# A fused attention and mixer kernel on one core: the row maxima of a query group by four products into one PSUM bank and one reduction, six visits to the value products in a group instead of seven, and the output products at other places

## The chip, the cores and the metric

One core of a Trainium2 chip runs the whole kernel. The metric is the device time of one execution in microseconds (us), the median of several runs. The engines are named as in the profile: PE (TensorE, with PEld for its weight loads), DVE (VectorE), ACT (ScalarE), POOL (GpSimd), and SP, which here issues DMAs only.

## The reference

`x` has 2048 tokens of 448 features; there are 16 query heads of 28 features, one shared key head and one shared value head.

```python
def _A_ref(x, wq, wk, wv, wo):
    q = (x @ wq).reshape(B, S, H, Dh).transpose(0, 2, 1, 3)
    k = x @ wk
    v = x @ wv
    scores = jnp.einsum("bhqd,bkd->bhqk", q, k) * (Dh ** -0.5)
    p = _softmax(scores, axis=-1)
    o = jnp.einsum("bhqk,bkd->bhqd", p, v)
    return o.transpose(0, 2, 1, 3).reshape(B, S, H * Dh) @ wo
def _B_ref(x, w1, w2, w3, w4):
    h = _gelu(_layernorm(x) @ w1)
    # four quarters of h, shifted by +1, -1, +2, -2 tokens, side by side: hs
    x1 = x + hs @ w2
    return x1 + _gelu(_layernorm(x1) @ w3) @ w4
g = _sigmoid((x * gate_w).sum(-1, keepdims=True))
out = g * _A_ref(x, ...) + (1 - g) * _B_ref(x, ...)
```

## The kernel before, in words

Three stages follow one another. In the first, the projections q, k, v and the first half of the mixer are computed. In the second, the mixer's wide MLP runs (`w3_part`, `w4_part`): for each block of 512 tokens, 14 slices of hidden features. The third stage is attention, and nearly all of the change lies there.

**Attention.** The work is cut into 16 groups `u` (4 blocks of 512 tokens by 4 groups of 4 heads). A group has 64 steps `at` = 4 kt + j: one per key tile `kt` (16 tiles of 128 keys) and head `j`. Step `at` is one score product on PE, called S below (S0 to S63 of a group): 128 keys by 512 queries into one PSUM bank. ACT then takes the exponential of that bank (one ACTIVATE) into an SBUF tile `p`.

**Values.** For each key tile, four products of `p` with the values accumulate into the bank `pv`, which stands apart from the others; they work side by side in four column strips of 32. They are not issued after each key tile but in visits: `VISITS = {kt: (lo, hi)}` says that after the scores of key tile `kt`, the value products of the tiles lo to hi - 1 (negative ones: of the group before) are issued. In the trace a key tile of values is eight MATMULs of line 870.

**Banks.** The score products go round seven PSUM banks in a fixed order: `bank()` takes the first of a list and puts it at the end. S therefore waits until whatever used its bank last has been read: by ACT, or by DVE where the bank held something else.

**Other PE work between the scores.** Three kinds of it:

- Output products (`wo_job`, W below): for the group before, four jobs of three products of 448 columns. A job takes the first bank off the list, holds it through its three products, puts it at the end of the list, and DVE then adds the bank to the output tile `ot` (line 824). `pump()` issues one product; `WO_AT` lists the steps at which it is called (`WO_LAST` in the last group).
- In the first group, four jobs of the same form (`w4_job`, at the steps `W4_AT`) finish the MLP's last hidden slice for the last 512 tokens. DVE adds their banks to `x1` (line 847). It needs `x1` of these tokens already multiplied by 1 - g, which POOL does in `weigh_x1(NT - 4, NT)` after it has cast and split the output weights (`woh`, `wol`, lines 830 and 831) that a DMA brings.
- Maxima (M below): a lower estimate of each query's largest score, taken over the first 32 keys, is subtracted in the scores of the next group through two extra rows of `qs`. Four products (one per 128 tokens, 128 columns each: 4 heads by 32 keys, `max_part`) each take a bank, and DVE reduces each (line 211). After the fourth, `max_end` does three small DVE operations, and SP sends the result to `qs` by four DMAs. For group 0 this is done within the second stage (`fills`).

After the last value product of a group, DVE copies `pv` to `o` (line 778), a DMA round trip spreads the reciprocal sums (`recip`), and `norm` (DVE, then POOL, lines 796 to 800) makes the operand of the output products.

All engines execute in the order in which the code is written.

Of the kernel before, what the change touches and what calls it, by code (L numbers as in the profile page):

```python
# [9 lines left out]
F32 = mybir.dt.float32  # L10
# [3 lines left out]
AX = mybir.AxisListType  # L14
PSUM = bass.MemoryType.PSUM

P = 128
# [3 lines left out]
DH = 28  # L21
# [3 lines left out]
NT = S // P  # L25
# [7 lines left out]
MK = 32  # L33
# [8 lines left out]
def gated_mix_kernel(  # L42
# [12 lines left out]
    nc = tc.nc  # L55
# [141 lines left out]
    NU = NB * NG  # L197
    q_of = {}
    qr_of, qh_of, ql_of = {}, {}, {}
    mx_of = {}  # L200
# [2 lines left out]
    def max_tile(name):  # L203
        return psA.tile([P, 512], F32, tag="mx", bufs=1, name=name)

    def max_part(u, t, tile_of):
        if t == 0:
            mx_of[u] = late.tile([P, 4, 4], F32, tag="mr", bufs=2, name=f"mr_{u}")
        ps = tile_of(f"m_{u}_{t}")[:, 0:4 * MK].rearrange("p (j k) -> p j k", j=4)
        nc.tensor.matmul(ps, qh_of[u][:, t * P:(t + 1) * P], khd[0:4 * DH], start=True, stop=True)  # L210
        nc.vector.reduce_max(mx_of[u][:, :, t], ps, axis=AX.X)  # L211

    def max_full(u, tile_of):
        mr = late.tile([P, 4, 4], F32, tag="mr", bufs=2, name=f"mf_{u}")
# [11 lines left out]
    def max_end(u):  # L226
        mr = mx_of.pop(u).rearrange("p j t -> p (j t)")
        mc = late.tile([P, 32], F32R, tag="mc", bufs=2, name=f"mc_{u}")
        nc.vector.tensor_scalar(mc[:, 0:16], mr, -1.0, None, op0=ALU.mult)
        nc.vector.scalar_tensor_tensor(mc[:, 16:32], mr, -1.0, f32(mc)[:, 0:16],  # L230
                                       op0=ALU.mult, op1=ALU.subtract)
        mrow = late.tile([P, 32], F32, tag="mrow", bufs=2, name=f"mrow_{u}")
        nc.vector.transpose(mrow, f32(mc))
        for p in range(4):
            nc.sync.dma_start(f32(qs_of[u % 2])[96:98, :, :].rearrange("k j (t p q) -> k p (j t) q", p=4, q=32)[:, p],
                              mrow[32 * p:32 * p + 32, :])
# [4 lines left out]
    with tc.tile_pool(name="s1b", bufs=1) as s1b, \  # L241
# [327 lines left out]
        late = ctx.enter_context(tc.tile_pool(name="late", bufs=1, side="right", reuse_waits="tile"))  # L569
        khd = late.tile([P, 4, MK], F32R, name="khd")  # L570
# [73 lines left out]
    with tc.tile_pool(name="s2", bufs=1, reuse_waits="tile") as s2, \  # L644
# [2 lines left out]
            for n in range(n0, n1):  # L647
                nc.gpsimd.tensor_scalar(x1[:, n, :], x1[:, n, :], gi[:, n:n + 1], None, op0=ALU.mult)

        fills = [lambda t=t: max_part(0, t, max_tile if t % 2 else misc_tile) for t in range(4)]  # L650
        fills += [lambda: max_end(0)]

        def fill():
            if fills:
# [84 lines left out]
    with tc.tile_pool(name="s3", bufs=1, reuse_waits="tile") as s3, \  # L739
# [121 lines left out]
        p_of, pv_of, sums, norms = {}, {}, [], []  # L861
# [10 lines left out]
            if kt == NT - 1 and u < NU - 1:  # L872
                sums.append(sums_begin(u, pv_of.pop(u)))

        WO_AT = (33, 36, 37, 40, 43, 44, 48, 50, 52, 53, 54, 55)
        M_AT = (5, 11, 17, 22)
        M_FIRST = (20, 29, 36, 40)
        W4_AT = (22, 29, 36, 37, 38, 41, 49, 50, 51, 54, 58, 61)
        WO_LAST = (36, 37, 38, 49, 50, 51)
        VISITS = {0: (-2, 0), 2: (0, 2), 4: (2, 4), 6: (4, 6), 8: (6, 8), 11: (8, 11), 14: (11, 14)}  # L880

        for k in range(NU * NT + 1):
            u, kt = divmod(k, NT)
            if k < NU * NT:
                if kt == 8 and 0 < u < NU - 1:
                    q_rows(u + 1)
                if kt == 13 and u + 2 < NU:
                    q_begin(u + 2)
                    q_fetch(u + 3)
                if kt == WO_AT[0] // 4 and u > 0:  # L890
                    for t in range(4):
                        jobs.append(wo_job(u - 1, t))
                if k == 0:
                    for t in range(4):
                        jobs.append(w4_job(t))
                pump_at = W4_AT if u == 0 else WO_AT if u < NU - 1 else WO_LAST
                p_of[k] = []
                for j in range(4):
                    n, at = 4 * k + j, 4 * kt + j
                    ps = bank(f"s_{n}")  # L900
                    nc.tensor.matmul(ps, kS[0:98, kt * P:(kt + 1) * P], q_of[u][0:98, j, :], start=True, stop=True)  # L901
                    p = s3.tile([P, 512], F32, tag="p", bufs=PB, name=f"p_{n}")
                    nc.scalar.activation(p, ps, AF.Exp, scale=SCALE)  # L903
                    p_of[k].append(p)
                    if at in pump_at:
                        pump()
                    if at == 12 and sums:
                        norms.append(recip(*sums.pop()))
                    if at == 27 and norms:
                        norm(*norms.pop())  # L910
                    m_at = M_AT if u else M_FIRST
                    if u + 1 < NU and at in m_at:
                        t = m_at.index(at)
                        max_part(u + 1, t, bank)
                        if t == 3:
                            max_end(u + 1)
            if k == NU * NT:
                while current[0] or jobs:
                    pump()
            lo, hi = VISITS.get(kt, (0, 0))  # L920
            for kk in range(u * NT + lo, u * NT + hi):
                if kk >= 0:
                    pv_group(kk)
        assert not sums and not norms

        u = NU - 1
# [155 lines left out]
```

## Time and profile before

| what | value |
|---|---|
| median of 3 runs | 957.29 us (957.19 to 958.32) |
| the profiled execution | 958.51 us, of which the span of its instructions 956.6 us |
| mean granted TensorE clock | 0.996 of full speed |
| busy over the span | PE 99%, ACT 68%, PEld 66%, DVE 29%, POOL 12% |
| attention's first score product, last exponential's start | 399.2 us, 940.6 us |

Times in the views are us from the start of the span. A PE row that is busy is not PE at its peak: matmuls are pipelined, so the distance from one start to the next is what a product costs, and the duration in the row is longer.

### The profile page before, as it was taken

How to read it: one execution, taken by the hardware profiler on the slowest of the kernel's cores; microseconds unless marked ns; L12 is line 12 of the kernel's file. 1: busy time of each engine (PE TensorE's matmuls, PEld its weight loads, DVE VectorE, ACT ScalarE, POOL GpSimd, SP SyncE). 2: the span in 40 equal slices, each digit the busy share in tenths (PEclk: the TensorE clock that was granted, in tenths of full speed). 3: DMA queues.
4: the chain of work that ended last, by engine and by line, in shares of the span. 5: the costliest groups of instructions: out<-in, count | busy, mean ns of one | idle time of the engine just before them, and what ended most of it. 6: DMA issues, size and time to landing. Idle time of an engine off the chain costs nothing.

```text
span 956.6 us, 13529 instructions
## 1 busy us (share of the span) xinstructions
PE 947.0 (99%) x5175; PEld 630.7 (66%) x5175; DVE 278.4 (29%) x573; ACT 648.3 (68%) x1266; POOL 116.5 (12%) x140
## 2 busy tenths in 40 slices
PE   9999999999999999999999999999999999999996
PEld 6788888888888888755555555455555555555543
DVE  5564454533423411221222122122221212212112
ACT  5542453322221222499999999999999999999994
POOL 3353300200002400040000000000000000000000
PEclk9999999999999999999999999999999999999998
DMA  9823452301300300111011021101111101210101
GB/s 308 279 70 90 131 165 84 84 10 29 83 2 1 83 1 10 38 51 42 23 40 48 16 79 51 38 21 46 52 52 40 52 16 37 89 42 13 31 13 42
DMA packets 45239, 57.33 MB, mean 60 GB/s; under 512 B 9856, under 2 KB 27968, under 8 KB 45168
## 3 DMA queue, kind: packets, MB, share of 16 engines
q1 hardware_dynamic: 41936, 50.47, 18.4%
q10 hardware_dynamic: 3168, 5.70, 1.7%
q8 instruction: 42, 0.69, 0.3%
q14 instruction: 29, 0.24, 0.1%
q0 software_dynamic: 64, 0.23, 0.1%
HBM read 32.19 MB, written 11.67 MB: 46 GB/s over the span
## 4 chain that ended last, share of the span: by engine, by line
PE 98%; DMA 1%; DVE 0%; ACT 0%; issue 0%; POOL 0%; POOLq 0%; ACTq 0%; SPq 0%
PE bank L901 28%; PE pv L870 25%; PE acc L678 5%; PE acc L680 5%; PE acc L679 5%; PE g L134 4%; PE g L135 4%; PE g L136 4%; PE bank L816 1%; PE bank L814 1%; PE bank L812 1%; PE g L137 1%; PE g L138 1%; PE h L134 1%; PE h L135 1%; PE h L136 1%
## 5 line engine op out<-in xcount | busy, mean ns | idle before, releaser
L903 ACT ACTIVATE p<-bank 128x512 f32<-128x512 f32 x1024 | 511.3, 643 | 32.9 <-PE bank L901 30.6
L901 PE MATMUL bank<-qs,kS 98*128 98x512 f32 x1024 | 305.8, 410 | 0.0
L901 PEld LDWEIGHTS bank<-qs,kS 98*128 98x128 f32 x1024 | 184.0, 189 | 134.3 <-issue 93.1
L870 PE MATMUL pv<-p,vext 128*32 128x512 f32 x2048 | 243.1, 598 | 0.0
L668 ACT ACTIVATE gh<-g 128x512 fp32r<-128x512 f32 x55 | 32.9, 598 | 184.5 <-PE g L138 184.5
L870 PEld LDWEIGHTS pv<-p,vext 128*32 128x32 f32 x2048 | 59.0, 109 | 114.6 <-issue 108.2
L670 DVE TENSOR_TENSOR gl<-gf,gh 128x512 fp32r<-128x512 f32 x55 | 38.2, 695 | 164.6 <-ACT gf L669 160.3
L678 PE MATMUL acc<-w4h,gh 128*128 128x448 f32 x220 | 80.2, 365 | 0.0
L680 PE MATMUL acc<-w4h,gl 128*128 128x448 f32 x220 | 80.0, 364 | 0.0
L679 PE MATMUL acc<-w4l,gh 128*128 128x448 f32 x220 | 79.9, 363 | 0.0
L824 DVE SCALAR_TENSOR_TENSOR ot<-bank,gg,ot 128x448 f32<-128x448 f32 x44 | 30.0, 684 | 146.2 <-ACT p L903 91.2
L799 POOL CAST onh<-on 128x512 fp32r<-128x512 f32 x15 | 9.1, 610 | 471.1 <-DVE on L796 471.1
L134 PE MATMUL g<-ah,w3h 128*128 128x512 f32 x168 | 65.8, 392 | 0.0
L135 PE MATMUL g<-al,w3h 128*128 128x512 f32 x168 | 65.7, 391 | 0.0
L136 PE MATMUL g<-ah,w3l 128*128 128x512 f32 x168 | 65.7, 391 | 0.0
L211 DVE TENSOR_REDUCE mr<-bank 128x4 f32<-128x128 f32 x60 | 17.6, 293 | 108.1 <-PE bank L210 108.1
L679 PEld LDWEIGHTS acc<-w4l,gh 128*128 128x128 f32 x220 | 41.3, 188 | 4.2
L678 PEld LDWEIGHTS acc<-w4h,gh 128*128 128x128 f32 x220 | 41.3, 188 | 4.2
L680 PEld LDWEIGHTS acc<-w4h,gl 128*128 128x128 f32 x220 | 41.3, 188 | 3.1
L778 DVE COPY o<-pv 128x512 f32<-128x512 f32 x15 | 10.4, 692 | 99.4 <-PE pv L870 99.4
L136 PEld LDWEIGHTS g<-ah,w3l 128*128 128x128 f32 x168 | 31.5, 188 | 7.0
L135 PEld LDWEIGHTS g<-al,w3h 128*128 128x128 f32 x168 | 31.5, 188 | 5.7
(195 smaller groups left out, 962.6 us busy)
## 6 DMA issues: line engine op xcount, KB each, us to landing
qs<-qh SPq DMA_DIRECT2D x32, 224.0 KB
qd<-qf ACTq DMA_DIRECT2D x16, 256.0 KB
rb<-rd SPq DMA_DIRECT2D x15, 256.0 KB
x<-in_x_dram SPq DMA_DIRECT2D x4, 896.0 KB
xd<-xt SPq DMA_DIRECT2D x16, 224.0 KB
w34raw<-in_w_dram SPq DMA_DIRECT2D x7, 512.0 KB
qr<-qd SPq DMA_DIRECT2D x16, 224.0 KB
qs<-ql SPq DMA_DIRECT2D x16, 224.0 KB
```

The costliest lines, as they stand in the source:

```text
L134: nc.tensor.matmul(ps, wh[:, c, :], ah[:, c, :], start=(c == 0), stop=False)
L135: nc.tensor.matmul(ps, wh[:, c, :], al[:, c, :], start=False, stop=False)
L136: nc.tensor.matmul(ps, wl[:, c, :], ah[:, c, :], start=False, stop=False)
L668: nc.scalar.activation(gh, ps, AF.Gelu_apprx_tanh)
L670: nc.vector.tensor_sub(gl, gf, f32(gh))
L678: nc.tensor.matmul(ps, gh[:, tok], w4h[i][:, k, :], start=(f == 0), stop=False)
L679: nc.tensor.matmul(ps, gh[:, tok], w4l[i][:, k, :], start=False, stop=False)
L680: nc.tensor.matmul(ps, gl[:, tok], w4h[i][:, k, :], start=False, stop=(f == stop))
L824: nc.vector.scalar_tensor_tensor(ot_of[n], ps, gg[:, n:n + 1], before, op0=ALU.mult, op1=ALU.add)
L870: nc.tensor.matmul(pv[32 * j:32 * j + 32, :], vext[:, kt, :], ps[j], start=(kt == 0), stop=(kt == NT - 1), tile_position=(0, 32 * j))
L901: nc.tensor.matmul(ps, kS[0:98, kt * P:(kt + 1) * P], q_of[u][0:98, j, :], start=True, stop=True)
L903: nc.scalar.activation(p, ps, AF.Exp, scale=SCALE)
```

## The change

The four maxima products of a group now stand in a row, each writing a quarter of the same bank, and one DVE reduction with 4 x 4 x 32 elements per partition reads them all; `max_end` follows at once. They stand at step 38 in every group. In the second stage, too, the five fill pieces become one.

```diff
-    def max_part(u, t, tile_of):
-        if t == 0:
-            mx_of[u] = late.tile([P, 4, 4], F32, tag="mr", bufs=2, name=f"mr_{u}")
-        ps = tile_of(f"m_{u}_{t}")[:, 0:4 * MK].rearrange("p (j k) -> p j k", j=4)
-        nc.tensor.matmul(ps, qh_of[u][:, t * P:(t + 1) * P], khd[0:4 * DH], start=True, stop=True)
-        nc.vector.reduce_max(mx_of[u][:, :, t], ps, axis=AX.X)
+    def max_first(u, tile_of):
+        mx_of[u] = late.tile([P, 4, 4], F32, tag="mr", bufs=2, name=f"mr_{u}")
+        ps = tile_of(f"m_{u}")[:, 0:16 * MK]
+        for t in range(4):
+            nc.tensor.matmul(ps[:, 4 * MK * t:4 * MK * (t + 1)], qh_of[u][:, t * P:(t + 1) * P], khd[0:4 * DH],
+                             start=True, stop=True)
+        nc.vector.reduce_max(mx_of[u].rearrange("p j t -> p t j"),
+                             ps.rearrange("p (t j k) -> p t j k", t=4, j=4), axis=AX.X)
+        max_end(u)
...
-        fills = [lambda t=t: max_part(0, t, max_tile if t % 2 else misc_tile) for t in range(4)]
-        fills += [lambda: max_end(0)]
+        fills = [lambda: max_first(0, misc_tile)]
...
-        WO_AT = (33, 36, 37, 40, 43, 44, 48, 50, 52, 53, 54, 55)
-        M_AT = (5, 11, 17, 22)
-        M_FIRST = (20, 29, 36, 40)
-        W4_AT = (22, 29, 36, 37, 38, 41, 49, 50, 51, 54, 58, 61)
+        WO_AT = (36, 37, 37, 38, 38, 39, 49, 50, 50, 63, 63, 63)
+        W4_AT = (22, 23, 24, 37, 38, 39, 49, 50, 51, 61, 62, 63)
         WO_LAST = (36, 37, 38, 49, 50, 51)
-        VISITS = {0: (-2, 0), 2: (0, 2), 4: (2, 4), 6: (4, 6), 8: (6, 8), 11: (8, 11), 14: (11, 14)}
+        M_AT = 38
+        VISITS = {1: (-3, 0), 3: (0, 3), 5: (3, 5), 7: (5, 7), 11: (7, 10), 14: (10, 13)}
...
-                    if at in pump_at:
+                    for _ in range(pump_at.count(at)):
                         pump()
-                    if at == 12 and sums:
+                    if at == 14 and sums:
                         norms.append(recip(*sums.pop()))
-                    if at == 27 and norms:
+                    if at == 29 and norms:
                         norm(*norms.pop())
...
+                    if u + 1 < NU and at == M_AT:
+                        max_first(u + 1, bank)
...
-            lo, hi = VISITS.get(kt, (0, 0))
+            lo, hi = VISITS.get(kt, (0, 0)) if k < NU * NT else (-3, 0)
```

Lines shift a little: the score product is line 902 after the change, the value product 872, the output products 814 to 818, the products of `w4_job` 843 to 847 and its DVE addition 849.

**First place: PE in group 0, around the last product of the first `w4_job`.** In the rows, `bank_0` to `bank_6` are the seven banks, `gl_late` is an operand of the third product of such a job, and the brackets name the engines waited for. Before:

```order
L901 MATMUL bank_6_3224<-qs0_1049,kS_75 128x512
L845 MATMUL bank_3_3221<-w4h_6_1504,gl_late_3174 128x448
L210 MATMUL bank_0_3218<-khd_1047,qh_1_3229 128x128
L901 MATMUL bank_1_3219<-qs0_1049,kS_75 128x512 [waits Activation_49]
L841 MATMUL bank_2_3220<-w4h_6_1504,gh_late_3173 128x448 [waits Activation_49]
L901 MATMUL bank_4_3222<-qs0_1049,kS_75 128x512 [waits Activation_49]
L843 MATMUL bank_2_3220<-w4l_6_1505,gh_late_3173 128x448
L901 MATMUL bank_5_3223<-qs0_1049,kS_75 128x512 [waits Activation_49]
L901 MATMUL bank_6_3224<-qs0_1049,kS_75 128x512 [waits Activation_49]
L210 MATMUL bank_3_3221<-khd_1047,qh_1_3229 128x128 [waits DVE_49]
```

After:

```order
L902 MATMUL bank_4_3216<-qs0_1049,kS_75 128x512
L847 MATMUL bank_2_3214<-w4h_6_1504,gl_late_3168 128x448
L902 MATMUL bank_5_3217<-qs0_1049,kS_75 128x512
L902 MATMUL bank_6_3218<-qs0_1049,kS_75 128x512 [waits Activation_49]
L902 MATMUL bank_0_3212<-qs0_1049,kS_75 128x512 [waits Activation_49]
L902 MATMUL bank_1_3213<-qs0_1049,kS_75 128x512 [waits Activation_49]
L902 MATMUL bank_3_3215<-qs0_1049,kS_75 128x512 [waits Activation_49]
L902 MATMUL bank_4_3216<-qs0_1049,kS_75 128x512 [waits Activation_49]
L902 MATMUL bank_2_3214<-qs0_1049,kS_75 128x512 [waits DVE_49]
```

The job's third product moved from behind S36 to behind S24, and the bank that it filled is asked for again by S31 (the last row), where before a maxima product behind S40 was the first to ask for it.

**Second place: PE in a middle group, around the maxima.** The names are those of group 10, whose maxima are for group 11. Before, one of the four maxima products:

```order
L901 MATMUL bank_4_3222<-qs0_1049,kS_75 128x512
L901 MATMUL bank_0_3218<-qs0_1049,kS_75 128x512
L901 MATMUL bank_1_3219<-qs0_1049,kS_75 128x512 [waits Activation_49]
L210 MATMUL bank_6_3224<-khd_1047,qh_11_6348 128x128 [waits Activation_49]
L901 MATMUL bank_2_3220<-qs0_1049,kS_75 128x512 [waits DVE_49]
L901 MATMUL bank_3_3221<-qs0_1049,kS_75 128x512 [waits Activation_49]
```

After, from the second product of the second output job (its bank is `bank_2`) at S38 to S46:

```order
L816 MATMUL bank_2_3214<-wol_3211,onh_9_6506 128x448
L210 MATMUL bank_0_3212<-khd_1047,qh_11_6311 128x128 [waits Activation_49]
L210 MATMUL bank_0_3212<-khd_1047,qh_11_6311 128x128 x3
L902 MATMUL bank_5_3217<-qs0_1049,kS_75 128x512 [waits Activation_49]
L818 MATMUL bank_2_3214<-woh_3210,onl_9_6507 128x448
L902 MATMUL bank_1_3213<-qs0_1049,kS_75 128x512 [waits Activation_49]
L902 MATMUL bank_3_3215<-qs0_1049,kS_75 128x512 [waits Activation_49]
L902 MATMUL bank_6_3218<-qs0_1049,kS_75 128x512 [waits DVE_49]
L902 MATMUL bank_4_3216<-qs0_1049,kS_75 128x512 [waits Activation_49]
L902 MATMUL bank_0_3212<-qs0_1049,kS_75 128x512 [waits DVE_49]
L902 MATMUL bank_5_3217<-qs0_1049,kS_75 128x512 [waits Activation_49]
L902 MATMUL bank_2_3214<-qs0_1049,kS_75 128x512 [waits DVE_49]
```

Three banks in eight steps now come back from DVE: the first job's at S42, the maxima's at S44 and the second job's at S46 (the last row).

**Third place: DVE in the same group.** Before, with `good`, `rr` and `on` belonging to the normalisation of group 9:

```order
L211 TENSOR_REDUCE mr_11_6440<-bank_2_3220 128x4 [waits PE_49]
L211 TENSOR_REDUCE mr_11_6440<-bank_6_3224 128x4 [waits PE_49]
L229 TENSOR_SCALAR mc_11_6524<-mr_11_6440 128x16 [waits DVE_49]
L230 SCALAR_TENSOR_TENSOR mc_11_6524<-mr_11_6440,mc_11_6524 128x16 [waits DVE_49]
L233 STREAM_TRANSPOSE mrow_11_6527<-mc_11_6524 128x32 [waits DMAHW5_49,DVE_49]
L796 TENSOR_TENSOR on_9_6548<-o_9_6430,rb_9_6480 128x512 [waits DMAHW3_49,Pool_49]
L824 SCALAR_TENSOR_TENSOR ot_8_6285<-bank_0_3218,gg_78,ot_8_6285 128x448 [waits PE_49,Activation_49]
L824 SCALAR_TENSOR_TENSOR ot_9_6311<-bank_6_3224,gg_78,ot_9_6311 128x448 [waits PE_49,Activation_49]
```

After:

```order
L798 TENSOR_TENSOR on_9_6504<-o_9_6406,rb_9_6436 128x512 [waits DMAHW3_49,DVE_49,Pool_49]
L826 SCALAR_TENSOR_TENSOR ot_8_6230<-bank_6_3218,gg_78,ot_8_6230 128x448 [waits PE_49,Activation_49]
L212 TENSOR_REDUCE mr_11_6554<-bank_0_3212 128x4x4 [waits PE_49,Activation_49]
L232 TENSOR_SCALAR mc_11_6560<-mr_11_6554 128x16 [waits DVE_49]
L233 SCALAR_TENSOR_TENSOR mc_11_6560<-mr_11_6554,mc_11_6560 128x16 [waits DVE_49]
L236 STREAM_TRANSPOSE mrow_11_6563<-mc_11_6560 128x32 [waits DMAHW7_49,DVE_49]
L826 SCALAR_TENSOR_TENSOR ot_9_6256<-bank_2_3214,gg_78,ot_9_6256 128x448 [waits PE_49]
```

The reduction and the three operations of `max_end` now stand between the additions of the first and the second output job, where before they stood ahead of both.

More of the change, by code (lines that the diff above doesn't have):

```diff
@@ L904, in gated_mix_kernel @@
                     p_of[k].append(p)
-                    if at in pump_at:
+                    for _ in range(pump_at.count(at)):
                         pump()
-                    if at == 12 and sums:
+                    if at == 14 and sums:
                         norms.append(recip(*sums.pop()))
-                    if at == 27 and norms:
+                    if at == 29 and norms:
                         norm(*norms.pop())
[L911 to L916, printed above, removed]
+                    if u + 1 < NU and at == M_AT:
+                        max_first(u + 1, bank)
             if k == NU * NT:
```

## The prediction

> **What bounds the kernel now.** I read the page first (engines, chain), then the lines of the attention stage, and then the timeline of one group.
>
> ```profile
> PE 947.0 (99%) x5175; PEld 630.7 (66%) x5175; DVE 278.4 (29%) x573; ACT 648.3 (68%) x1266; POOL 116.5 (12%) x140
> ...
> PE 98%; DMA 1%; DVE 0%; ACT 0%; issue 0%; POOL 0%; POOLq 0%; ACTq 0%; SPq 0%
> ...
> L903 ACT ACTIVATE p<-bank 128x512 f32<-128x512 f32 x1024 | 511.3, 643 | 32.9 <-PE bank L901 30.6
> L901 PE MATMUL bank<-qs,kS 98*128 98x512 f32 x1022 | 305.3, 410 | 0.0
> ```
>
> The chain is PE almost throughout. In attention, ACT's idle time before the exponentials (32.9 us) is nearly all put down to PE (30.6), and PE's own idle time is nil: PE sets the pace, ACT follows closely. So whatever PE issues counts in full, and whatever makes PE wait counts too. One group, from the timeline:
>
> ```profile
> 604.80 0.69 DVE L778 COPY o<-pv 128x512 f32<-128x512 f32 x1 [6.93 <-PE pv L870]
> 612.69 0.96 PE L901 MATMUL bank<-qs,kS 98*128 98x512 f32 x3
> 613.49 0.23 PE L210 MATMUL bank<-khd,qh 112*128 112x128 f32 x1
> 613.55 1.37 PE L901 MATMUL bank<-qs,kS 98*128 98x512 f32 x5
> 613.75 0.29 DVE L211 TENSOR_REDUCE mr<-bank 128x4 f32<-128x128 f32 x1 [3.02 <-PE bank L210]
> 614.08 0.17 DVE L229 TENSOR_SCALAR mc<-mr 128x16 fp32r<-128x16 f32 x1
> 614.29 0.17 DVE L230 SCALAR_TENSOR_TENSOR mc<-mr,mc 128x16 fp32r<-128x16 f32 x1
> 614.50 0.21 DVE L233 STREAM_TRANSPOSE mrow<-mc 128x32 f32<-128x32 f32 x1
> 614.63 0.65 DVE L796 TENSOR_TENSOR on<-o,rb 128x512 f32<-128x512 f32 x1
> 623.85 0.37 PE L816 MATMUL bank<-woh,onl 128*128 128x448 f32 x1
> 624.05 0.96 PE L901 MATMUL bank<-qs,kS 98*128 98x512 f32 x3
> 624.33 0.68 DVE L824 SCALAR_TENSOR_TENSOR ot<-bank,gg,ot 128x448 f32<-128x448 f32 x1 [1.57 <-PE bank L816]
> 624.51 0.19 PEld L901 LDWEIGHTS bank<-qs,kS 98*128 98x128 f32 x1 [0.27 <-ACT p L903]
> 624.94 2.78 PE L870 MATMUL pv<-p,vext 128*32 128x512 f32 x24
> 627.65 0.50 PE L901 MATMUL bank<-qs,kS 98*128 98x512 f32 x1
> 629.99 0.40 PE L901 MATMUL bank<-qs,kS 98*128 98x512 f32 x1
> 630.87 1.10 PE L901 MATMUL bank<-qs,kS 98*128 98x512 f32 x4
> 634.61 2.13 PE L901 MATMUL bank<-qs,kS 98*128 98x512 f32 x8
> 636.67 1.92 PE L870 MATMUL pv<-p,vext 128*32 128x512 f32 x16
> 638.53 0.73 PE L901 MATMUL bank<-qs,kS 98*128 98x512 f32 x2
> 638.74 0.69 DVE L778 COPY o<-pv 128x512 f32<-128x512 f32 x1 [6.92 <-PE pv L870]
> ```
>
> A group takes 638.74 - 604.80 = 33.94 us. Prices, start to start: a score product (1.10 - 0.40)/3 = 0.233. An output product 624.05 - 623.85 = 0.20. A visit: two key tiles take 638.53 - 636.67 = 1.86, three 627.65 - 624.94 = 2.71, so 0.85 a tile and 0.16 for any visit; the eight scores ahead, 636.67 - 634.61 = 2.06, are 0.19 more than 8 x 0.233. **A visit's fixed price is 0.35 us.** A maxima product between scores: from the last score before it (612.69 + 0.96 - 0.40 = 613.25) to the last after it (613.55 + 1.37 - 0.40 = 614.52) it is 1.27, five scores are 1.165, so 0.105.
>
> **The change, part by part.**
>
> *Visits.* Seven a group (six in the first) and one at the end were 112; six a group (five in the first) and one at the end are 96. Each group gains 0.35.
>
> *Maxima in a row.* The trace has no two such products together. Bounds for one behind another: the 0.06 from 613.49 to 613.55 below, a score's 0.233 above. I take 0.11, the same product's price between scores, its nearest row. [...]
>
> ```profile
> L210 PEld LDWEIGHTS bank<-khd,qh 112*128 112x128 f32 x60 | 11.3, 188 | 2.1
> ```
>
> So four in a row cost what four apart cost, within 0.02. Were a whole load of 188 ns paid for each, the sum would be 15 x 3 x 0.078 = 3.5 us higher. [...]
>
> *One reduction of 512 elements.* Not in the trace. Bounds: 0.29 (row of 613.75, 128 elements) and four times that, 1.17. I take 0.69, DVE's copy of 512 elements out of PSUM (row of 604.80). DVE has the time; what matters is who queues behind it. That is the addition of the second output job, whose bank S46 wants. From the first maxima product, at 0: fourth product 0.33; reduction from 0.33 + 0.26 (613.49 to 613.75) = 0.59 to 1.28; the three operations of max_end and the hand-over, 0.59 (from 614.04, the end of the reduction, to 614.63), to 1.87; addition 0.68, to 2.55; 0.05 to answer the wait and 0.10 for the weight load, so 2.70. PE without a wait: S39 at 0.44, the job's third product at 0.67, S40 at 0.88, S46 at 0.88 + 6 x 0.233 = 2.28. **S46 waits 0.42 us.** Behind it on PE are S47, a visit and all the rest. The maxima's own bank (S44, 1.81 against 1.28 + 0.15) and the first job's are back in time. Their price per product drops out of this wait: it delays both sides.
>
> A wait of 0.1 at the old S47 goes: its weight load came at 624.51, held up by ACT, so that the product could start at 624.61, not at 624.05 + 2 x 0.233 = 624.52. Middle groups: -0.35 + 0.42 - 0.1 + 0.05 (one old maxima product stood ahead of a visit and cost less) = +0.02, **14 groups +0.3**, in effect nothing.
>
> *The first group.* Its rows:
>
> ```profile
> 399.20 3.53 PE L901 MATMUL bank<-qs,kS 98*128 98x512 f32 x12
> 417.44 0.37 PE L845 MATMUL bank<-w4h,gl_late 128*128 128x448 f32 x1
> ...
> 399.63 17.83 ACT L903 ACTIVATE p<-bank 128x512 f32<-128x512 f32 x36 [2.69 <-PE bank L901]
> ...
> 411.00 1.68 POOL L830 CAST woh<-woraw 128x1792 fp32r<-128x1792 f32 x1 [12.63 <-DMA woraw<-in_wo_dram]
> 412.76 4.04 POOL L831 TENSOR_TENSOR wol<-woraw,woh 128x1792 fp32r<-128x1792 f32 x1
> 416.78 5.56 POOL L648 TENSOR_SCALAR x<-x,gi 128x448 f32<-128x448 f32 x4
> ...
> 418.22 0.68 DVE L847 SCALAR_TENSOR_TENSOR x<-bank,gi,x 128x448 f32<-128x448 f32 x1 [4.04 <-POOL x L648]
> ```
>
> Before, the first late job ended at 417.44, and its addition started at 418.22, when POOL had weighed the first x1 tile (416.78 + 5.56/4 = 418.17). POOL hangs on a DMA, not on PE, and the change moves nothing ahead of it on SP or POOL. Now the job ends behind S24. Where is that? Scores now run 16 in a stretch; from S9 on they take ACT's pace, 17.83/36 = 0.49, as the stretched 3.53 of the twelve shows. S8 at 399.20 + 1.87, S15 at 404.3 (S9 a little early), a visit of three tiles, S16 at 407.4; seven scores and two job products, 2.4 with the step to the visit, its two tiles 1.86: S24 at 411.7. S25 to S30 follow, and S31, on the job's bank, would start 0.1 + 0.2 + 7 x 0.233 later, at 413.6. The addition cannot start before 418.2; the bank is back at 418.22 + 0.68 + 0.15 = 419.05. **S31 waits 5.5 us**, and PE, in order, does nothing else. The first group: -0.35 (a visit), -0.85 (a tile moved to the end), +1.0 (S12 to S15 at ACT's pace, 4 x 0.26), +5.5, and, with small waits exchanged, +0.1: **+5.4**.
>
> *The last group and the end.* Visits after key tiles 7 and 11 leave 16 scores and three products between them, with no maxima to slow PE. S47 would be at 0.34 + 14 x 0.233 + 0.6 = 4.2 from S32, but its bank holds S40's scores, whose exponential starts 0.6 + 8 x 0.48 = 4.4 and is over, with 0.15, at 5.25: a wait of 1.0, less 0.35 for the visit. At the end three tiles instead of two follow the last scores, +0.85. **Together +1.5.**
>
> *Second stage.* One fill instead of five: the same four products on PE, DVE busy 1.3 us in one piece; the slice's gl is used two slices later, so it is covered. Nothing. Were that cover gone, 1 us once.
>
> *PE's clock behind the 5.5 us.* PE idles nowhere for so long before; the nearest rows are the tail, by windows (PEclk is the figure behind the engines):
>
> ```profile
> 943.00:945.00 2.00, 1.37 (x6) 0.84 (x6) 1.10 (x5) 0.91 (x6) 0.00 (x0) 1.00 0.00 0
> 945.00:946.00 1.00, 0.69 (x3) 0.50 (x4) 0.87 (x6) 0.50 (x3) 0.00 (x0) 1.00 0.00 0
> 946.00:948.00 2.00, 2.00 (x8) 1.57 (x7) 1.23 (x4) 0.27 (x1) 0.00 (x0) 0.52 0.00 0
> 948.00:950.00 2.00, 2.00 (x8) 1.55 (x6) 1.02 (x3) 0.63 (x1) 1.15 (x1) 0.63 0.31 115
> ```
>
> After three sparse microseconds the granted clock falls to 0.52 and 0.63 for some four: 2 x 0.48 + 2 x 0.37 = **1.7 us** of PE work. I add it, bounds 0 and 3.4. [...]
>
> **Sum.** 0.3 + 5.4 + 1.5 + 1.7 = +8.9. The profiled execution took 958.5 (a span of 956.6 and 1.9 around it), so 967.4; it lies 1.2 above the median, 957.3, so for the median **966.2**.
>
> **Rivals.**
>
> [...]
> 2. *Only one of the two DVE waits.* With a reduction of 0.29 the S46 wait is gone: 966.2 - 15 x 0.4 = 960.2. With POOL done before 413.6 the S31 wait and the clock loss go: 966.2 - 7.2 = 959. Against the latter: POOL's rows hang on the DMA's landing.
> 3. *Faster: DVE answers in time at both places.* Then visits rule: 16 x -0.35, -1.5 for the old waits at S47, +1.0 + 1.0 for scores at ACT's pace, +0.8 for the rest: -4.3, 953. It decides if the chain behind the fourth maxima product is 0.42 us shorter and POOL 4.6 us earlier. For: DVE is 71% idle. Against: the row at 418.22, which already waited for POOL with the job twelve steps later.
> 4. *Dearer maxima*: 0.233 a product, 15 x 3 x 0.12 = +5.5, and a reduction of 1.17, 15 x 0.48 = +7.2: either gives 972 to 973.
>
> **How the numbers follow.** A measurement here tells 0.2% from no change, 1.9 us. Chances: forecast 0.45; rival 1 0.25; rival 2 0.12; rival 3 0.07; rival 4 0.07; around no change, when several sizes err together, 0.04. Range 960 to 971.5: it reaches down to rival 2 and stops short of rival 4; outside lie rivals 3 and 4 and no change. Faster 0.07, same 0.04, slower 0.89.
>
> **What would show it.** In the trace after: one wait of PE near 413 to 419 in the first group, at a score product released by DVE, and ACT idle as long; PEclk below 1 after it; in each further group a wait of about 0.4 at one score behind the maxima, released by DVE, group time near 33.95, ACT idle behind the four visits of three tiles instead of two; one reduction near 0.69. It is wrong if S31's bank is free by 414, or if the four maxima products take 0.2 each.

## The result, and the profile after

The changed kernel takes 975.2 us (median of 5 runs, 972.3 to 976.4), the kernel before 958.3 beside it: a ratio of 1.0176, 95% interval 1.0162 to 1.0189. It is slower, as forecast, but by 16.9 us and not by 8.9, and the time lies above the range.

The profiled execution of the changed kernel is the shortest of its five, 972.29 us, 13.8 above the profiled one of before. So the sums below explain 13.8, and the median is treated near the end of the section on the prediction. Most of it lies in attention. From the first exponential's start to the last one's it took 540.9 us before and 555.8 after. By groups, from exponential to exponential:

| | first group | mean of the 14 middle groups | last group |
|---|---|---|---|
| before | 33.60 | 33.96 | 31.86 |
| after | 39.49 | 34.51 | 33.11 |
| difference in all | +5.9 | +7.7 | +1.25 |

The page's rows of the exponentials and the scores (busy, mean ns of one, then the idle time ahead and what ended it):

```profile
L904 ACT ACTIVATE p<-bank 128x512 f32<-128x512 f32 x1024 | 509.4, 643 | 49.7 <-PE bank L902 49.6
L902 PE MATMUL bank<-qs,kS 98*128 98x512 f32 x1024 | 291.4, 409 | 7.9 <-DVE x L849 4.5
```

ACT's idle time rose from 32.9 to 49.7, by 16.8, and its busy time fell by 1.9: together the 14.9 that the stage grew. The scores, which never waited before, now wait 7.9 us themselves. Who makes PE and its weight loads wait, in the attention stage (total us, times, longest; a weight load and its product wait in part for the same thing, so the rows aren't to be added):

```profile
PE bank L902 <- DVE x L849: 4.5, 1, 4.5
PE bank L902 <- DVE ot L826: 3.4, 14, 0.5
PE bank L818 <- POOL onl L802: 1.4, 4, 0.5
...
PEld bank L902 <- DVE ot L826: 9.5, 14, 0.9
PEld bank L818 <- POOL onl L802: 7.0, 14, 0.9
```

The first is the first group's S31, the second S46 of each middle group; both were forecast. The third was not: the third output product (line 818, the one that reads `onl`) waits for POOL, in all 14 middle groups. Weight loads of scores wait for ACT as well, 43.5 us in all and 9.5 before, but 38.6 of the 43.5 are first loads behind a visit, which waited before, too, and stand under "issue" there.

**First group.** Timeline rows of PE, DVE and POOL, and the windows of the clock (the figure behind the five engines):

```profile
412.02 1.55 PE L902 MATMUL bank<-qs,kS 98*128 98x512 f32 x6
418.05 0.80 PE L902 MATMUL bank<-qs,kS 98*128 98x512 f32 x1 [4.47 <-DVE x L849]
...
417.31 0.68 DVE L849 SCALAR_TENSOR_TENSOR x<-bank,gi,x 128x448 f32<-128x448 f32 x1 [16.40 <-POOL x L651]
...
415.87 5.55 POOL L651 TENSOR_SCALAR x<-x,gi 128x448 f32<-128x448 f32 x4
...
416.00:420.00 4.00, 1.96 (x9) 0.69 (x13) 0.68 (x1) 0.60 (x1) 4.00 (x3) 0.74 0.00 0
420.00:424.00 4.00, 4.00 (x21) 2.00 (x14) 0.00 (x0) 1.53 (x4) 1.42 (x2) 0.83 0.00 0
```

S30 starts at 412.02 + 1.55 - 0.40 = 413.17, so S31 could have started at 413.40; it started at 418.05, a wait of 4.65. Its bank waits for DVE, DVE for POOL's first x1 tile. Behind it PE runs at a granted clock of 0.74 and 0.83, that is 4 x 0.26 + 4 x 0.17 = 1.7 us lost. Counted from its first score product instead of its first exponential, the group grew by 6.4: ACT was 1.3 us behind PE at its end before, and is 0.8 behind after.

**Middle groups.** The chain of waits, followed back from the end, no longer stays on PE. In group 14, the longest of the middle groups with 35.4 us, it leaves it twice (start, us, what):

```profile
887.90 2.76 PE pv L872 x24
890.68 0.70 DVE o L780
891.40 1.90 DMA rt<-o
893.69 2.29 DMA rd<-rr
896.00 7.35 DMA rb<-rd
903.47 0.70 DVE on L798
904.30 0.62 POOL onh L801
904.99 1.29 POOL onl L802
906.32 0.47 PE bank L818
906.79 0.25 PE bank L902
907.25 0.66 DVE ot L826
907.95 0.70 DVE mr L212
909.31 0.58 DVE ot L826
909.93 0.74 PE bank L902 x2
```

From the last value product to the third output product there is now a path that PE waits for: copy, sums out, reciprocals out, the broadcast of 256 KB back (`rb`, 7.35 us), the product, POOL's two operations. Then it goes on through DVE: an output job's addition, the reduction (0.70), the second addition, and S46 with S47 behind it.

Why is the broadcast late? SP's queue, before and after, in a middle group:

```profile
609.29 0.58 SPq L791 DMA_DIRECT2D rb<-rd  x1
614.77 2.69 SPq L235 DMA_DIRECT2D qs<-mrow  x4
617.51 0.88 SPq L195 DMA_DIRECT2D qs<-qh  x1
```

```profile
619.66 0.57 SPq L793 DMA_DIRECT2D rb<-rd  x1
620.32 0.89 SPq L195 DMA_DIRECT2D qs<-qh  x1
...
622.17 0.81 SPq L195 DMA_DIRECT2D qs<-qh  x1
```

Before, SP stood at the four small DMAs of the maxima (`qs<-mrow`) until DVE had them ready, and the three query-row DMAs of 224 KB each came 8.2 us behind the broadcast. Now the maxima come later in a group, their DMAs stand behind the query rows, nothing holds SP, and the rows go out 0.66 us behind the broadcast. From its issue to DVE's product that reads it took 5.0 to 5.4 us before, and 7.1 to 7.8 after, but 5.0 in the last group, which has no query rows to fetch.

### The profile page after: what moved, and what is told of

It reads as the page before. It is cut to its first block, busy times and chain, and to the rows that moved or that the text cites. A ratio compares the mean times of both kernels' runs of the same rounds, so it can differ in the third digit from the quotient of the medians.

```text
span 970.5 us, 13412 instructions
## 1 busy us (share of the span) xinstructions
PE 951.5 (98%) x5175; PEld 627.6 (65%) x5175; DVE 270.8 (28%) x525; ACT 646.4 (67%) x1266; POOL 116.1 (12%) x140
## 5 line engine op out<-in xcount | busy, mean ns | idle before, releaser
L904 ACT ACTIVATE p<-bank 128x512 f32<-128x512 f32 x1024 | 509.4, 643 | 49.7 <-PE bank L902 49.6
L902 PE MATMUL bank<-qs,kS 98*128 98x512 f32 x1024 | 291.4, 409 | 7.9 <-DVE x L849 4.5
L902 PEld LDWEIGHTS bank<-qs,kS 98*128 98x128 f32 x1024 | 183.7, 188 | 134.1 <-ACT p L904 43.5
L670 ACT ACTIVATE gh<-g 128x512 fp32r<-128x512 f32 x55 | 32.9, 598 | 184.7 <-PE g L138 184.7
L798 DVE TENSOR_TENSOR on<-o,rb 128x512 f32<-128x512 f32 x15 | 10.4, 693 | 130.5 <-DMA rb<-rd 130.5
L134 PEld LDWEIGHTS g<-ah,w3h 128*128 128x128 f32 x168 | 31.5, 188 | 5.6
```

Of the source, the lines that this page charges most:

```text
L134: nc.tensor.matmul(ps, wh[:, c, :], ah[:, c, :], start=(c == 0), stop=False)
L670: nc.scalar.activation(gh, ps, AF.Gelu_apprx_tanh)
```

## The experiments

Times move by up to 2.6 us between executions for a reason in the first 11 us (last section), so the attention stage and its groups are compared beside the medians. "Broadcast" is the time from SP's issue to DVE's product, in the groups that fetch rows behind it.

| kernel | median us | ratio to before, 95% interval | attention | first | middle | last | broadcast |
|---|---|---|---|---|---|---|---|
| before | 957.3 to 958.5 | | 540.9 | 33.60 | 33.96 | 31.86 | 5.0 to 5.4 |
| after | 975.2 | 1.0176, 1.0162 to 1.0189 | 555.8 | 39.49 | 34.51 | 33.11 | 7.1 to 7.8 |
| rows late | 969.4 | 1.0116, 1.0090 to 1.0141 | 550.4 | 40.24 | 34.08 | 33.11 | 4.9 to 5.5 |
| late jobs | 970.7 | 1.0118, 1.0092 to 1.0144 | 554.5 | 35.26 | 34.72 | 33.12 | 7.1 to 8.4 |
| maxima at 40 | 971.0 | 1.0124, 1.0092 to 1.0155 | 555.3 | 40.82 | 34.39 | 33.08 | 7.2 to 8.4 |
| all three | 958.7 | 0.9993, 0.9980 to 1.0006 | 539.3 | 32.88 | 33.81 | 33.12 | 4.9 to 5.4 |
| before, rows early | 962.1 | 1.0039, 1.0025 to 1.0054 | 545.8 | 33.61 | 34.31 | 31.85 | 7.1 to 8.6 |
| all three, maxima at 34 | 954.5 | 0.9958, 0.9942 to 0.9974 | 536.3 | 32.67 | 33.61 | 33.11 | 4.8 to 5.5 |
| before, visits alone | 981.7 | 1.0250, 1.0221 to 1.0279 | 564.1 | 34.68 | 35.46 | 33.07 | 4.7 to 5.4 |
| before, maxima alone | 959.4 | 1.0009, 0.9996 to 1.0021 | 542.0 | 33.69 | 34.04 | 31.81 | 5.4 to 6.2 |
| one row DMA (one run) | 970.6 | | 551.2 | 40.65 | 34.10 | 33.08 | 5.7 to 6.2 |
| rows first (one run) | 988.4 | | 569.1 | 40.29 | 35.41 | 33.08 | 4.8 to 5.4 |

**Query rows later.** The changed kernel with

```diff
-                if kt == 8 and 0 < u < NU - 1:
+                if kt == 11 and 0 < u < NU - 1:
                     q_rows(u + 1)
```

> The changed kernel, with the three DMAs of q_rows issued at key tile 11 instead of 8. Theory A (in the changed kernel these 224 KB transfers stand right behind the broadcast rb on SP's queue, where before the four DMAs of the maxima held them back; they slow rb, so DVE's on, POOL's onl and the third output product come late): rb to on falls from 7.2 to 8.5 us to about 5.3, the products at S37 no longer wait for POOL, 0.3 to 0.4 a group, 14 groups: 4 to 6 us less than the changed kernel, about 970. Theory B (the chain from o to the output products is simply too short now, whatever else is on the queues): on stays at 7 us or more behind rb, the time stays at 975.

The broadcast is back at 4.9 to 5.5 us, no output product waits for POOL any more, and a middle group fell from 34.51 to 34.08: 14 x 0.43 = 6.0 us, as the medians say too (975.2 to 969.4). DVE's product, which starts when the broadcast has landed, in the group whose broadcast SP issued at 620.80:

```profile
625.93 0.69 DVE L798 TENSOR_TENSOR on<-o,rb 128x512 f32<-128x512 f32 x1 [6.62 <-DMA rb<-rd]
```

What stays in a middle group is 34.08 - 33.96 = +0.12: a visit less (-0.35), the wait of S46 and S47 (+0.50), and the forecast's two small terms (-0.1 and +0.05) make +0.10.

**Late jobs later.** The changed kernel with

```diff
-        W4_AT = (22, 23, 24, 37, 38, 39, 49, 50, 51, 61, 62, 63)
+        W4_AT = (36, 37, 37, 38, 38, 39, 49, 50, 50, 63, 63, 63)
```

> The changed kernel, with W4_AT put at the places of WO_AT, so that the first late job ends at S37, when POOL has nearly weighed its tile. Theory (PE's single wait in the first group, 4.9 us in the trace, with the clock of 0.74 and 0.83 behind it, costs about 6.6): 968.5. Rival (ACT, not PE, sets the first group's time there, and the wait is half made up): no more than 3 us less, 972.

The 4.65 us wait is gone, and the clock at its old place is granted in full (1.00 from 412 to 424 us). The first group fell by 4.2 to 35.26 instead of by 6.6, for two reasons. There, too, the reduction now queues on DVE among the jobs' additions, and S46 starts 0.8 later for it. And in this execution the clock fell earlier in the group, behind the first sixteen scores, so that a visit of three tiles took 4.48 us instead of the 2.78 of the changed kernel, 1.7 more:

```profile
404.49 4.48 PE L872 MATMUL pv<-p,vext 128*32 128x512 f32 x24
...
404.00:408.00 4.00, 4.00 (x22) 1.22 (x25) 0.00 (x0) 3.44 (x8) 0.00 (x0) 0.59 0.91 236
```

Together they are the 2.4 by which this group is longer than with all three edits (32.88). The median fell by 4.6. The same sixteen scores are in the other kernels with the six visits, and the changed kernel was granted 1.00 in the same stretch; why the clock fell here isn't known.

**Maxima two steps later.** The changed kernel with

```diff
-        M_AT = 38
+        M_AT = 40
```

> The changed kernel, with M_AT = 40: the reduction and max_end stand behind both additions on DVE. Theory (S46 waits 0.4 to 0.5 us a group for the second addition): the wait at S46 is gone, 15 x 0.45 = 6.8 less, 968.5. Rival (the output products' wait for POOL or the next bank takes its place): less than 2 us less, 973.5 or more.

The wait of S46 for DVE is gone altogether, so the reduction among the jobs' additions was its cause. But the gain was 4.2 us by the medians, not 6.8. In this execution the broadcast took 7.2 to 8.4 us, and the waits for POOL are longer than in the changed kernel (7.0 there in the first row, 1.1 in the second):

```profile
PEld bank L818 <- POOL onl L802: 10.0, 14, 0.9
...
PEld bank L814 <- POOL onh L801: 4.2, 7, 0.9
```

**All three.** The three edits together.

> The changed kernel with all three edits. If the three waits are separate and nothing new comes up: 975.2 - 5 - 6.6 - 6.8 = 957, group time about 33.6 in the trace. By the prices of the prediction (its third rival, both DVE waits gone) 953. Rival (the waits overlap or new ones appear): 960 or more.

The losses are gone: 958.7, the time of before. By the medians the three single repairs gain 5.8, 4.6 and 4.2, together 14.6 of the 16.6 that they gain at once. No wait for DVE or POOL is left. But it isn't faster, although a group has a visit less. What is left stands at S42 to S47, weight loads of scores that wait for ACT, 0.3 us a group:

```profile
PEld bank L902 <- ACT p L904: 50.4, 90, 0.8
```

**Maxima at 34.** The same with

```diff
-        M_AT = 40
+        M_AT = 34
```

> The three repairs together, with the maxima at step 34 instead of 40, ahead of the first output product and not among them. What was left in the middle groups with the three repairs were waits of scores 42 to 47 on ACT, 0.3 us a group: the reduction at step 40 holds a bank of the seven for as long as two output jobs hold theirs. Theory (banks held together by DVE leave too few for ACT's queue): with the reduction done before the first job ends, these waits fall below 0.05, middle groups go from 33.81 to about 33.6, 14 x -0.2 = -3, the first group loses about 0.4, and the time is about 955 (0.996 to 0.997 of before). Rival (ACT's own pace over sixteen scores sets those waits, wherever the maxima stand): the groups stay at 33.8 and the time at 958.5. Second rival: DVE's product of the sums, at step 29, is still waiting for its broadcast when the reduction queues behind it, and a score waits for the maxima's bank: groups 34 or more.

```profile
L904 ACT ACTIVATE p<-bank 128x512 f32<-128x512 f32 x1024 | 508.6, 647 | 31.0 <-PE bank L902 31.0
...
PEld bank L902 <- ACT p L904: 44.3, 68, 0.8
```

Faster than both kernels, 954.5, ratio 0.9958. The waits fell from 90 to 68, a middle group from 33.81 to 33.61, ACT's idle time from 34.1 to 31.0. What remains in the second row are mostly the first loads behind a visit (47 of the 68, 39.4 us), whose price is the visit's; the others fell from 11.0 to 4.8 us. So those waits weren't ACT's own pace; with the maxima's bank and two output jobs' banks held at once for DVE, four of seven are left for scores. A middle group now is 0.35 shorter than before. The forecast's price of a visit with its two small terms (-0.1 and +0.05) gives 0.40, so the price holds to within 0.05.

**Visits alone.** The kernel before with the six visits (and the steps 14 and 29 of the sums and their product, and three tiles in the last visit) of the change:

```diff
-        VISITS = {0: (-2, 0), 2: (0, 2), 4: (2, 4), 6: (4, 6), 8: (6, 8), 11: (8, 11), 14: (11, 14)}
+        VISITS = {1: (-3, 0), 3: (0, 3), 5: (3, 5), 7: (5, 7), 11: (7, 10), 14: (10, 13)}
```

> The kernel before with the six visits of the change alone (and the sums and their product two steps later, as the change has them); maxima and output products stay where they were. By the prediction's price of 0.35 us a visit, and nothing else, 16 x -0.35 = -5.6, 953. Rival (the visits' gaps are what gives ACT time: sixteen scores in a stretch, with output products thinner than in the change, run PE into ACT's pace of 0.49 us a score): walking a group step by step with 0.233 a score, 0.20 an output product, 0.105 a maxima product and 0.49 of ACT gives 35.3 instead of 33.9 for a middle group, +1.4 x 15 = +20 or more, 975 to 982.

By itself, the part that the forecast priced at 5.6 us of gain costs 23.2 us in attention. The reading is in ACT's row (before: 32.9 idle), in the waits of the weight loads for ACT (before: 9.5, 46 times, none over 0.3; of the 72.6 here 38.6 are first loads behind a visit, the other 34.8 are to be compared), and in ACT's timeline:

```profile
L903 ACT ACTIVATE p<-bank 128x512 f32<-128x512 f32 x1024 | 510.2, 647 | 57.3 <-PE bank L901 55.6
...
PEld bank L901 <- ACT p L903: 72.6, 167, 0.8
...
609.70 5.99 ACT L903 ACTIVATE p<-bank 128x512 f32<-128x512 f32 x12 [0.94 <-PE bank L901]
```

ACT needs 64 x 0.49 = 31.4 of a group's 33.96 us (0.49 from 17.83 us for 36 in the first group before); 2.5 are to spare. With seven banks PE can be ahead of it by no more than about seven scores. In a stretch of sixteen, PE runs into that limit and stands; behind it, in a visit of three tiles, ACT runs dry, for 0.8 us (the row shows 0.94, behind a stretch of twelve): each idles for the other in turn. With the change's output products, which stand close together in the long stretch and slow PE down towards ACT's pace, the same six visits gain (the kernel with the maxima at 34). So the parts can't be priced apart. That it is the places of the output products that make the difference is inferred: no run moved them alone.

**Maxima alone.** The kernel before with four products into one bank and one reduction at step 22 (40 in the first group), all else as before:

```diff
-                    m_at = M_AT if u else M_FIRST
-                    if u + 1 < NU and at in m_at:
-                        t = m_at.index(at)
-                        max_part(u + 1, t, bank)
-                        if t == 3:
-                            max_end(u + 1)
+                    if u + 1 < NU and at == (22 if u else 40):
+                        max_first(u + 1, bank)
```

> The kernel before with the four maxima products into one bank and one reduction alone, at step 22 (step 40 in the first group), the places where the fourth product stood; visits and output products as before. By the prediction's prices (four in a row cost what four apart cost, one reduction of 0.69 in place of four of 0.29, and no output product near) nothing: 958 +- 2, the middle groups at 33.9 to 34.0; the first group may lose up to 4 us if the reduction, queued on DVE behind the addition that waits for POOL, holds its bank longer than the seven banks last. By the rival of dearer maxima (0.233 a product): +5.5, 964.

No difference that can be told (0.9996 to 1.0021); middle groups 0.08 longer, the first not 4 us longer but 0.1. The prices of the products and the reduction hold; dearer maxima are excluded. The broadcast's 5.4 to 6.2 here is no landing time: DVE is busy with the maxima then and comes to the product later.

**Before, with the rows early.** One line of the kernel before:

```diff
-                if kt == 8 and 0 < u < NU - 1:
+                if kt == 5 and 0 < u < NU - 1:
                     q_rows(u + 1)
```

> The kernel before with one line changed: the three DMAs of the query rows are issued at key tile 5 instead of 8, so that they stand on SP right behind the broadcast of the reciprocal sums, as they did after the change. Theory A (DMAs issued behind the broadcast slow it): the distance from SP's issue of the broadcast to DVE's product that reads it rises from 5.2 to about 7.2 us in the middle groups and stays at 5.2 in the last one, which has no such DMAs. Theory B (the broadcast is slower after the change for another reason, the engine or the group's new visits): it stays at 5.2. The time under A: in the kernel before the first output product stands at step 33 and the fifth score after it is some 2 us away from the broadcast's landing, so PE may wait up to 1 us a group at the output products; between 958 and 970. Under B 958.5.

The broadcast went to 7.1 to 8.6 us in a kernel that has nothing else of the change, and stayed at 5.1 in the last group: the order on SP is the cause, not the visits or the maxima. It costs 4.4 us, through a wait that the kernel before doesn't have at all:

```profile
PE bank L812 <- POOL onh L799: 2.8, 4, 1.0
...
PEld bank L812 <- POOL onh L799: 6.5, 10, 1.4
```

**One row DMA behind the broadcast.** The changed kernel with one of the three left at key tile 8, the other two at 11:

```diff
-                    q_rows(u + 1)
+                    q_rows(u + 1, 0, 1)
+                if kt == 11 and 0 < u < NU - 1:
+                    q_rows(u + 1, 1, 3)
```

> The kernel after the change with one of the three query-row DMAs (224 KB) left behind the broadcast at key tile 8, the other two moved to key tile 11. So far: none behind it 5.1 us from SP's issue to DVE's product, three 7.2 and more. Theory A1 (the broadcast shares the transfer engines with whatever is issued behind it): one DMA costs about a third of three, 5.6 to 6.0 us, and as much spread. Theory A2 (any DMA behind it costs the whole, or it is a matter of order): 7 us. Theory A3 (only a long queue delays it): 5.1. The wait of the third output product under A1: the chain has 1.9 us of room after the change, so it is gone in nearly all groups, and the middle groups are at 34.1 as with all three late.

```profile
621.13 0.57 SPq L793 DMA_DIRECT2D rb<-rd  x1
621.79 0.87 SPq L195 DMA_DIRECT2D qs<-qh  x1
...
626.98 0.69 DVE L798 TENSOR_TENSOR on<-o,rb 128x512 f32<-128x512 f32 x1 [7.34 <-DMA rb<-rd]
```

5.7 to 6.2 us: one costs a third of what three cost, and PE waited for `onl` only once. The transfers share; it is no matter of order as such. The packets of 2 KB show it, too: with rows late, where the broadcast runs alone, they took 87 ns each (132 in 5.2 us, 13.8% of 16 engines; in the kernel before 90 ns, 132 in 5.2 us, 14.2%), and in the changed kernel 146 ns (445 in 7.4 us, 54.9%).

**Rows between the sums and the reciprocals.** The changed kernel with

```diff
-                if kt == 8 and 0 < u < NU - 1:
+                if kt == 3 and 0 < u < NU - 1:
                     q_rows(u + 1)
```

> The kernel after the change with the three query-row DMAs issued at key tile 3, ahead of the sums and of their broadcast on SP, instead of key tile 8, behind it. If what counts is that the transfers run at the same time: the rows are under way for about 4 us when the broadcast is issued; three of 224 KB at the 250 GB/s that the windows show take 2.7 us, so they are through by then: 5.1 us from issue to product, no wait of output products, middle groups 34.1. If three DMAs anywhere near the broadcast in SP's queue slow it, 7 us and groups of 34.5. A second risk: the small transfer of the sums stands behind the rows in the queue, so the chain ahead of the broadcast (4.5 us from DVE's copy to the issue of the broadcast) grows by 1 to 2 us, which the 1.9 us of room would just about cover.

```profile
623.95 0.60 SPq L782 DMA_DIRECT2D rt<-o  x1
624.60 0.89 SPq L195 DMA_DIRECT2D qs<-qh  x1
...
627.35 0.48 SPq L791 DMA_DIRECT2D rd<-rr  x1
630.71 0.60 SPq L793 DMA_DIRECT2D rb<-rd  x1
```

At key tile 3 the rows are not ahead of the sums' transfer (`rt`), as the expectation has it, but right behind it and ahead of the reciprocals (`rd`) and the broadcast. The broadcast itself is at 4.8 to 5.4 again, but the two small transfers `rt` and `rd` now run beside the rows, and `rd` queues behind their issue: from `rt` to `rb` it takes 6.8 us instead of 3.75, and the time is the worst of all, 988. The second risk of the expectation came true, at 3.0 us where 1 to 2 were priced.

## Why the prediction was right and wrong

- **S31 and POOL: right.** The place, the engine and the cause were as forecast; the wait was 4.65 instead of 5.5, because POOL began to weigh at 415.87, 0.9 earlier than in the execution of before. Why it came earlier wasn't traced.
- **The clock behind it: right in kind**, and rival 1, no loss of clock, falls: in all five kernels that have this wait the clock fell (0.50 to 0.84 by windows in two, 0.8 to 0.9 over a slice of the page in the other three; last section). That its size came out at 1.7 us is partly luck. In rows late the three windows from 416 to 428 us show 0.81, 0.50 and 0.84, about twice the loss of clock, of which 4 x 0.50 + 4 x 0.16 = 2.6 us came after S31 had started at 420.00, and its first group took 40.24 instead of 39.49 (40.3 to 40.8 in the other three). The clock can also fall without such a wait, as in the late-jobs kernel.
- **S46: right**, 0.40 and another 0.10 at S47, against 0.42. The maxima-at-40 kernel shows the cause. The old wait of 0.1 at S47 is read a little wrong: the score itself started at 624.52, and the visit behind it came 0.1 late; the size stands. No run shows the 0.10 for the weight load that the sum has behind the addition: in the changed kernel S31 and S46 started at most 0.01 behind their loads and 0.06 behind the end of DVE's addition (417.99 to 418.05, 633.22 to 633.28).
- **Maxima and reduction: right.** Four products from 630.63 to the score at 631.03 and a reduction of 0.70, against 0.69. The four take 0.10 each in a row, against the 0.11 that was put in. The reduction of 128 elements took 0.29 before, so four times the elements take 2.4 times as long and not four times. That a reduction takes as long as DVE's copy of 512 elements out of PSUM was the author's estimate, and for this one it held.
- **Visits: right in price, 0.35** against 0.40 with the small terms, once the waits were gone (the kernel with the maxima at 34). That the price can be added up visit by visit is not so: with the visits alone the kernel lost 23 us.
- **Last group and end: the wait was there.** Nine scores in a row take 3.30 us in place of 2.33 before, 1.0 more, and the last visit has its third tile, 2.78 us:

```profile
927.19 2.33 PE L901 MATMUL bank<-qs,kS 98*128 98x512 f32 x9
```

```profile
940.96 3.30 PE L902 MATMUL bank<-qs,kS 98*128 98x512 f32 x9
...
955.58 2.78 PE L872 MATMUL pv<-p,vext 128*32 128x512 f32 x24
```

  By the exponentials the group grew by 1.25 where 0.65 was expected. From first to last score product it is 32.10 before and 32.72 after, +0.62: the other 0.6 is that the group's first exponential came 1.5 us behind its score before and comes 0.8 behind it after. The third tile cost its 0.85, but the end is not longer: from the first to the last start of the twelve output products behind the last visit it took 3.99 us before, from 945.73 at the clock of 0.52 and 0.63 that the prediction shows, and 2.44 after, from 961.29 at 1.00. So the stretch from the last exponential's start to the end is 0.8 us shorter (16.1 to 15.3), by the luck of the clock.
- **The step that failed: "Middle groups: -0.35 + 0.42 - 0.1 + 0.05 = +0.02, 14 groups +0.3, in effect nothing".** One term is missing from it. The forecast moved `max_end` on PE and DVE and never on SP, though its four DMAs were what kept the query rows away from the broadcast, nor did it follow the path from the last value product to the third output product. The rows of that path, from DVE's copy of `pv` to the end of `onl` and to the third output product (means of 13 groups): before, 12.6 and 16.8, so 4.2 us of room. In the kernel with rows late, 12.5 and 14.4: the change alone brings the product 2.4 us closer. It stands at step 37 as before, but the last value product of the group before now comes behind key tile 1 instead of 0, so four scores (0.93), a visit with one tile (0.35 + 0.85) and the four maxima products (0.42) no longer stand between; 1.9 of room would have done. After, the path takes 14.7: the broadcast needs some 2 us more and the room is gone. The wait is 0.4 us a group in the profiled execution (0.04 at the first product, 0.26 at the third, 0.10 at the next score). With it, and with 0.50 in place of 0.42, the sum is -0.35 + 0.50 - 0.1 + 0.05 + 0.40 = +0.50, where +0.55 was measured. The rows-late kernel shows the term by itself: 0.43 a group.
- **Size.** First group +5.9, middle groups +7.7, last +1.25, less 1.0 at the two ends, makes the 13.8 of the profiled executions, to 0.1. The forecast had +7.1, +0.3 and +1.5 with the end. Why the median is 3 us higher than the profiled execution stays open; three things are on record. The broadcast: where two other executions with rows behind it were profiled (late jobs, maxima at 40), it took up to 8.4 us, and groups ran from 33.8 to 35.5. The clock: its mean was 0.992 to 0.996 in the other four runs and 0.997 in the profiled one, and in rows late the clock lost behind the start of S31 was 2.6 us instead of 1.7, some 1 us more. The start: the profiled execution was one of the fast ones there (last section), which is worth up to 2.6 us.
- **The rivals.** Both waits on DVE came, so the second rival falls; the products and the reduction were not dearer, so the fourth does. The faster one asked that DVE answer in time at both places. That point was right as far as it goes: with both and the broadcast repaired and the maxima ahead of the jobs the kernel takes 954.5, where 953 was worked out. But it needed a third condition that nobody had named.

## What to carry to other kernels

When work is moved, follow each of its DMAs through the issuing queue: an instruction that waits there spaces out the transfers behind it, and moving it lets a large one run beside a small one that somebody waits for (here the rows came 0.66 us behind the broadcast instead of 8.2, and the broadcast took 7.1 to 7.8 us instead of 5.0 to 5.4). Before costing a move at nothing, take the whole path between producer and consumer (here values, sums, broadcast, POOL, product), its length and its room, from the rows; a path with 4 us of room before may have 2 after the move and none after the next. Where two engines run at nearly the same pace with a few banks between them, the number of stretches and the filler in them act together, and a price per visit holds only while neither runs into the other (here the six visits by themselves cost 23.2 us in attention, and a middle group gained 0.35 us by them with the other output products and the maxima at 34).

## What the runs showed of the hardware

- A broadcast load of 256 KB from DRAM took about 5.1 us from SP's issue to its reader; with one 224 KB DMA issued 0.66 us behind it on the same queue 5.9, with three 7.1 to 8.6. By the usual 7.3 with three that is some 0.75 us for each. So what was issued later delayed what was issued first, about in proportion to the number of DMAs: by 0.8 us with one, by some 2.2 with three.
- Behind PE's one long wait (4.4 to 4.9 us in five kernels) the granted clock fell, in one execution for two windows of 4 us (0.74, 0.83), in rows late for three (0.81, 0.50, 0.84). With the maxima at 40, one row DMA and the rows first, the slice of the page around the end of the wait, 24 to 25 us long, reads 8 (0.8 to 0.9) where its neighbours read 9. In the late-jobs execution it fell to 0.59 from 404 to 408 us, where no row of PE shows a wait and its sixteen scores only ran at ACT's pace (5.49 us).
- The first eight products of the kernel take 3.70 us in the execution of before that was profiled, 5.38 with rows late and 6.28 with all three, from nearly the same start, and all that follows is later by as much. The code there is the same:

```profile
5.20 3.70 PE L305 MATMUL q<-xkv,wqraw 128*128 128x512 f32 x8 [0.81 <-DMA wqraw<-in_wq_dram]
```

```profile
5.16 6.28 PE L308 MATMUL q<-xkv,wqraw 128*128 128x512 f32 x8 [0.53 <-DMA wqraw<-in_wq_dram]
```

  The trace's record of the granted clock has its first entry, at full clock, at 3.99 us in the first and at 10.39 in the second; up to there most products stand some 0.85 us apart, behind it 0.43. In the twelve profiled executions that entry comes between 3.99 and 10.39, and attention's first exponential starts at 399.4 to 399.7 in the six where it comes by 5.4, and at 402.1 in the one where it comes last. So 2.6 us, more than most of the effects here, can come from the first microseconds of an execution; what sets that moment wasn't tested.
